# Output product with 4-column stationary loads, and heads 0 to 4 of wo loaded last, one transfer each

## The chip, the cores and the metric

One core of one Trainium2 chip. The metric is the device time of one execution in microseconds (us). A profiled or timed execution also has a *span*: from the first to the last of the program's own instructions, less than its time by 1.6 to 1.9 us in the kernel before.

## The reference

```python
# one decode step, batch 4, D = 448; 16 query heads on 8 KV heads, 8192 cached keys, head size 256
xn = layernorm(A_x)
q  = (xn @ wq)                                   # 448 x 4096
p  = softmax(q . k_cache / 16)                   # 32 pairs (batch, KV head): 4 MB of K and 4 MB of V each
o  = p . v_cache
s  = o.reshape(4, 1, 4096) @ wo                  # the "output product": 4096 x 448
g  = silu(B_ref(xn, w1, w2, w3, w4))             # a small MLP
out = A_x + s * g                                # 4 x 1 x 448, bf16
```

279 MB are read to compute 1792 numbers.

## The kernel before

One queue (SP, SyncE) issues all large loads in order: weights, K and V of 32 heads, and wo. Most of wo (`NLATE` and up) comes early; the heads in `LATE` come last, behind all of V. The last head's V comes in four pieces.

```python
LATE = ((0, 1), (2,), (3,))              # heads of wo at the end of the stream, by transfer
NLATE = sum(len(g) for g in LATE)
...
load_wo(NLATE, HQ, "dwo")                # early, between the first K loads
for h in range(2, NH):
    load_k(h); load_v(h - 2)
load_v(NH - 2)
load_v(NH - 1)                           # the last head's V, in pieces of 32, 16, 8, 8
for i, hs in enumerate(LATE):
    load_wo(hs[0], hs[-1] + 1, "dwl%d" % i)
```

At the end TensorE finishes attention and multiplies by wo. Heads `NLATE` to 13 are done while V still comes in (`f_ou`). The rest is this (`DQ` = 224, `NDG` = 2, `PQ` = 32, `Bn` = 4; OT holds the attention output with its 4 batch columns padded to 32):

```python
def f_o(hs, stop=False):
    for hq in hs:
        for dh in range(NHALF):
            for i in range(NDG):         # two groups of 224 columns: a "pair" of matmuls
                ins = pe.matmul(o_ps[i * PQ:(i + 1) * PQ, 0:DQ],
                                OT[:, hq // REP, hq % REP, dh, :],          # stationary, 32 columns
                                wo_sb[:, hq, dh, i * DQ:(i + 1) * DQ], ...) # moving, 224 columns
...
f_direct(NPIECE - 1).then_inc(S["p_pv"], 1)      # last piece of V; VectorE then writes the last OT
take(pe, "dwl0", 16)                             # wait for a landing
f_o(LATE[0])
take(pe, "v_ot")                                 # wait for the last OT (heads 14 and 15)
f_o(range(HQ - REP, HQ))
for i in range(1, len(LATE)):
    take(pe, "dwl%d" % i, 16)
    ins = f_o(LATE[i], i == len(LATE) - 1)
ins.then_inc(S["p_o"], 1)                        # VectorE: times silu, plus x; then the store
```

In each head's body TensorE transposes K, so it waits for K's landing at the top of the body. That is its one long idle stretch per head (28 such waits in the trace of before, 76.3 us together, the longest 4.6 us).

## Time and profile before

| | |
|---|---|
| time | 657.61 us median (657.61 to 658.3, 3 runs) |
| span of the profiled execution | 656.9 us |
| HBM | 278.99 MB, 425 GB/s over the span |

In the page's slices (the span in 40 equal parts, tenths of full) the DMA engines are busy at 90% or more from the second slice to the last but one.

```profile
PEclk9698999887899878889987888988878987887998
DMA  8999999999999999999999999999999999999996
```

So the load stream sets the pace, and only what comes after its end can be won or lost by an engine. The timeline of the last microseconds (start us, duration us, engine, line, operation; in brackets the idle time before it and what ended it):

```profile
649.21 0.55 PE L697 MATMUL pst<-pT,kn 128*128 128x32 bf16 x16 [0.19 <-PEq L245]
...
650.56 0.56 PE L697 MATMUL pst<-pT,kn 128*128 128x32 bf16 x16
651.27 0.18 DVE L520 TENSOR_TENSOR OT<-pst,rz 128x4 bf16<-128x4 f32 x1 [1.79 <-DVEq L245]
651.58 2.01 PEld L687 LDWEIGHTS pst<-wo_sb,OT 128*32 128x32 bf16 x24 [0.57 <-issue]
651.61 2.41 PE L687 MATMUL pst<-wo_sb,OT 128*32 128x224 bf16 x24 [0.50 <-PEq L245]
654.06 0.38 DVE L526 TENSOR_TENSOR res<-pst,sg 64x224 f32<-64x224 f32 x1 [2.61 <-PE pst L687]
654.47 0.38 DVE L528 TENSOR_TENSOR out_b<-res,x 64x224 bf16<-64x224 f32 x1
```

L697 is the direct product on the last two pieces of V, L520 writes the last OT, L687 is `f_o`. Its 24 matmuls end at 654.02. The chain that ended last consists of these and nothing earlier (start, duration, what):

```profile
651.61 2.42 PE pst L687 x24
...
654.06 0.39 DVE res L526
```

The DMA issues in the last 42 us: operation, KB, us from issue to landing; and the SP queue's timeline.

```profile
wo_sb<-in_A_wo_dram SPq DMA_DIRECT2D x1, 448.0 KB, 29.5
wo_sb<-in_A_wo_dram SPq DMA_DIRECT2D x2, 224.0 KB, 29.6
```

```profile
621.96 11.71 SPq L229 DMA_DIRECT2D wo_sb<-in_A_wo_dram  x3
```

The first of the three is issued at 621.96 and lands 29.5 us later, at 651.48; by the trace's landing records the others land at 652.03 and 652.59. Nearly all of the 11.71 us of issuing is the third issue (10.7 us). Seven earlier transfers had not landed even at its end, and no other issue on this queue took over 0.6 us. No record names the cause.

Last, busy times of the engines in two stretches. The third number from the end is TensorE's granted clock:

```profile
620.00:627.00 7.00, 5.88 (x92) 5.70 (x93) 2.59 (x5) 2.98 (x7) 0.00 (x0) 0.76 1.00 431
...
651.70:653.40 1.70, 1.70 (x20) 1.64 (x21) 0.00 (x0) 0.00 (x0) 0.00 (x0) 0.50 0.02 8
```

The output product ran at half clock.

### The profile page before, as it was taken

The page shows a single profiled execution, that of the slowest core. Times are in us where ns is not written, and L with a number is a line of the kernel's source. Part 1 is how long each engine was busy: PE and PEld are TensorE (multiplying, and loading weights), DVE is VectorE, ACT ScalarE, POOL GpSimd, SP SyncE. Part 2 cuts the span into 40 slices and gives each one's busy share as a digit, 9 for nine tenths or more (in the row PEclk, how much of TensorE's full clock was granted, in tenths as well). Part 3 has the DMA queues.
Part 4 walks back from the last instruction along what each step waited for, and adds up shares of the span by engine and source line. Part 5 has one row for each costly group of instructions (what it writes and reads, how often), then busy time and mean ns, then how long its engine had stood idle before and what let it go on. Part 6 is the DMA issues. An engine that isn't in the chain of part 4 may idle for free. (4 is left out here: it accounts for less than half of the span.)

```text
span 656.9 us, 22864 instructions
## 1 busy us (share of the span) xinstructions
PE 556.3 (85%) x9937; PEld 476.3 (73%) x9937; DVE 276.5 (42%) x589; ACT 256.0 (39%) x364; POOL 13.4 (2%) x77
## 2 busy tenths in 40 slices
PE   1899997988888988888897888898888889888897
PEld 0487886876766887667787766798767678766775
DVE  7353554443443444434443443444334443433442
ACT  4144544442433443323444333444333344433340
POOL 2000000000000000000000000000000000000000
PEclk9698999887899878889987888988878987887998
DMA  8999999999999999999999999999999999999996
GB/s 360 440 413 425 434 427 437 425 439 427 437 427 435 429 435 431 431 435 427 437 429 433 429 433 429 433 429 433 429 435 431 433 431 435 429 433 433 429 425 256
DMA packets 12353, 279.13 MB, mean 425 GB/s; under 512 B 1204, under 2 KB 3256, under 8 KB 3768
## 3 DMA queue, kind: packets, MB, share of 16 engines
q1 hardware_dynamic: 12328, 278.99, 99.2%
q8 instruction: 7, 0.11, 0.1%
q14 instruction: 2, 0.02, 0.0%
q10 hardware_dynamic: 16, 0.01, 0.0%
HBM read 278.99 MB, written 0.00 MB: 425 GB/s over the span
## 5 line engine op out<-in xcount | busy, mean ns | idle before, releaser
L588 PE MATMUL pst<-ident_b,kn 128*128 128x128 bf16 x4096 | 347.3, 239 | 78.6 <-PEq L245 76.3
L295 ACT ACTIVATE kT<-pst 128x1024 bf16<-128x1024 bf16 x224 | 229.3, 1024 | 360.6 <-ACTq L245 359.5
L588 PEld LDWEIGHTS pst<-ident_b,kn 128*128 128x128 bf16 x4096 | 275.4, 108 | 84.3 <-issue 83.8
L293 DVE COPY kT<-pst 128x1024 bf16<-128x1024 bf16 x288 | 197.5, 691 | 263.7 <-DVEq L245 263.7
L600 PE MATMUL psc<-qc,kT 128*128 128x2 bf16 x4096 | 178.7, 165 | 0.0
L600 PEld LDWEIGHTS psc<-qc,kT 128*128 128x128 bf16 x4096 | 157.7, 98 | 28.5 <-issue 28.3
L639 PE MATMUL psv<-vb,pT 128*4 128x512 bf16 x1056 | 86.4, 378 | 0.3 <-issue 0.3
L618 PE MATMUL psm<-sel,po 128*128 128x2 f32 x272 | 36.8, 257 | 0.5 <-PEq L245 0.5
L618 PEld LDWEIGHTS psm<-sel,po 128*128 128x128 f32 x272 | 34.8, 197 | 0.9 <-issue 0.9
L639 PEld LDWEIGHTS psv<-vb,pT 128*4 128x4 bf16 x1056 | 22.3, 82 | 15.3 <-issue 0.8
L452 DVE TENSOR_REDUCE rmax<-psc 128x2 f32<-128x128 f32 x32 | 9.3, 292 | 48.8 <-DVEq L245 48.8
L470 DVE COPY po<-psv 128x512 f32<-128x512 f32 x34 | 23.5, 692 | 3.0 <-DVEq L245 2.3
L457 DVE TENSOR_REDUCE gmax<-psm 2x1 f32<-2x128 f32 x32 | 8.9, 279 | 34.7 <-DVEq L245 34.7
L317 ACT ACTIVATE pT<-psc,negb 128x64 bf16<-128x64 f32 x66 | 20.6, 331 | 5.4 <-ACTq L245 5.4
L612 PEld LDWEIGHTS psm<-diag,ones_f 2*128 2x128 f32 x66 | 14.1, 263 | 6.4 <-issue 5.4
L280 POOL COPY qc<-qT 128x4 bf16<-128x4 bf16 x32 | 5.9, 186 | 585.8 <-DVEq L469 568.6
L612 PE MATMUL psm<-diag,ones_f 2*128 2x2 f32 x66 | 16.8, 321 | 1.1 <-PEq L245 0.9
L317 ACT ACTIVATION_READ_ACCUMULATOR pT<-psc,negb 128x1 f32 x66 | 13.6, 206 | 0.0
L608 PEld LDWEIGHTS psm<-ident_f,rmax 128*2 128x2 f32 x32 | 2.6, 80 | 14.0 <-issue 14.0
L536 PE MATMUL pst<-ident_b,xn_b 4*128 4x4 bf16 x14 | 0.6, 161 | 13.6 <-DVE xn_b L365 8.9
L630 PE MATMUL psm<-rowsum,ones_f 128*128 128x2 f32 x64 | 11.6, 251 | 0.0
L536 PEld LDWEIGHTS pst<-ident_b,xn_b 4*128 4x128 bf16 x14 | 0.5, 100 | 13.6 <-issue 8.9
(101 smaller groups left out, 122.4 us busy)
## 6 DMA issues: line engine op xcount, KB each, us to landing
kn<-in_A_k_cache_dram SPq DMA_DIRECT2D x32, 4096.0 KB, 25.7
vb<-in_A_v_cache_dram SPq DMA_DIRECT2D x31, 4096.0 KB, 31.3
vb<-in_A_wq_dram SPq DMA_DIRECT2D x1, 3584.0 KB, 11.7
vb<-in_B_w_dram SPq DMA_DIRECT2D x2, 1568.0 KB, 16.6
wo_sb<-in_A_wo_dram SPq DMA_DIRECT2D x1, 2688.0 KB, 44.3
kn<-in_A_v_cache_dram SPq DMA_DIRECT2D x1, 2048.0 KB, 25.2
kn<-in_A_v_cache_dram SPq DMA_DIRECT2D x1, 1024.0 KB, 27.3
kn<-in_A_v_cache_dram SPq DMA_DIRECT2D x2, 512.0 KB, 28.5
```

Source lines behind the costliest of these rows:

```text
L293: engine.tensor_copy(dst, src).then_inc(S["v_ev"], 1)
L295: engine.activation(dst, src, ACT.Copy).then_inc(S["a_ev"], 1)
L317: ins = act.activation(pv_p[:, :, hh], sc[:, :, hh], ACT.Exp, bias=negb[:, s, hh:hh + 1], scale=SCALE, accum_out=rowsum[:, s, hh:hh + 1])
L452: v.tensor_reduce(rmax[:, :], psc[h % 2][:, 0:NCH * REP].rearrange("p (k h) -> p h k", h=REP), AX.X, ALU.max).then_inc(S["v_rmax"], 1)
L457: v.tensor_reduce(gmax[:, :], psm[0:REP, 0:P], AX.X, ALU.max).then_inc(S["v_s"], 1)
L470: v.tensor_copy(po[:, slot], psv[:, 0:CP * DH]).then_inc(S["v_po"], 1)
L588: ins = pe.transpose(dst[:, t * P:(t + 1) * P], kn[:, h % 2, GC * j + kl, half * P:(half + 1) * P], ident_b[:, :])
L600: ins = pe.matmul(psc[h % 2][:, kk * REP:(kk + 1) * REP], kT[:, j % RING, t * P:(t + 1) * P], qc[:, h % 2, half, :], start=(half == 0), st ...
L612: pe.matmul(psm[:, P:P + REP], ones_f[0:REP, :], diag[:, :], start=True, stop=True).then_inc(S["p_m2"], 1)
L618: ins = pe.matmul(dst(dh)[:, 0:width], po[:, slot, i * DH + dh:(i + 1) * DH:NHALF], sel[:, i, 0:width], start=(i == 0), stop=(i == CP - 1))
L630: pe.matmul(psm[:, P + REP:P + 2 * REP], ones_f[:, :], rowsum[:, h % 2, :], start=True, stop=True)
L639: ins = pe.matmul(psv[o:o + CP * REP, 0:CP * DH], pT[:, h % 2, kk * REP:(kk + CP) * REP], src[:, kk:kk + CP, :].rearrange("p c d -> p (c d)"),
```

## The change

Two things. The output product loads 4 stationary columns in place of 32, the padding being zero. And head 4 of wo moves from the early load to the end, where five heads now come in a transfer each, so that the product can follow the landings head by head.

```diff
-    LATE = ((0, 1), (2,), (3,))
+    LATE = ((0,), (1,), (2,), (3,), (4,))
@@ f_o
-                            ins = pe.matmul(o_ps[i * PQ:(i + 1) * PQ, 0:DQ],
-                                            OT[:, hq // REP, hq % REP, dh, :],
+                            ins = pe.matmul(o_ps[i * PQ:i * PQ + Bn, 0:DQ],
+                                            OT[:, hq // REP, hq % REP, dh, 0:Bn],
```

`LATE[0]` runs ahead of the wait for the last OT, all else behind it. Before, `LATE[0]` was two heads, and 16 matmuls stood behind the wait (heads 14, 15, 2, 3). After, it is one head, and 24 stand behind it (14, 15, 1, 2, 3, 4).

## The prediction

> **What bounds the kernel now.** The load stream. The page's slices show the DMA engines at 90% or more from the second slice to the last but one, 425 GB/s over the span. So only the end counts; the chain of waits starts at 651.6 us of the 656.9 us span.
>
> The last transfers land (records of the trace) one behind the other: the last piece of V at 650.37 us, heads 0 and 1 of wo at 651.48, head 2 at 652.03, head 3 at 652.59. That is 1.11 us for two heads and 0.555 us for one: 224 KB at about 413 GB/s, with no visible fixed cost per transfer. The output product's 24 matmuls (the timeline's line L687) start at 651.61 and end at 654.02, so they outlast the last landing by 1.4 us. From 651.67 us the granted clock is 0.50, and a pair (two column groups of 224 columns, side by side) then starts every 187 ns.[...] The pair's pace is thus the moving operand's, not the weight load's.
>
> **Stationary loads of 4 columns.** [...]In the trace the loads (146 ns) are issued ahead and hidden; what shows is the stagger of 33 ns between the two matmuls of a pair; with 4 columns (attention's product has such loads) it is 3 to 4 ns. I expect the pace of 187 ns to stay and about 0.03 us to be saved, once, at the end.
>
> **Five transfers, one head each.** The bytes don't change; head 4 (224 KB) moves from the early bulk to the end. All K and V land about 0.54 us earlier (the last piece of V at 649.83). The steps between 640 and 651 us each start within some 0.1 us of a landing, so they move along, and the last OT (now 651.44) comes at about 650.9. The end of the stream stays at 652.6, or up to 0.1 us later for two more transfers. Head 0 is now done before OT is there; heads 14 and 15 run from 651.05 at the full clock (until it drops), heads 1, 2 and 3 soon after landing, and only head 4's two pairs remain after the last landing. After the last landing: 0.135 us to the first matmul (as before), 0.19 to the second pair, 0.39 for its latency: the product ends near 653.3, against 654.02. Were the clock at half from 651.05, twelve pairs would end at 653.55. Saved: 0.5 to 0.85 us, all on the critical path. The tail after it only moves.
>
> **Predicted time:** 656.9 us, range 656.0 to 658.0. Faster by over 2%: 0.01; within 2%: 0.98; slower: 0.01.
>
> **What would show it.** Last V piece 0.5 us earlier, last wo landing within 0.15 us of 652.6, landings of wo 0.55 us apart; 28 matmuls on the product's line, pace 187 ns at half clock with a stagger of a few ns; an idle gap on TensorE before the last heads, ended by a landing; end of the product near 653.3.
>
> **What would make it wrong.** The third wo transfer's issue already took 10.7 us[...]. Two more may stall longer; if the fifth is queued only after about 650 us the stream gets a hole and the end comes later. The clock may drop earlier. The runs before differ by 0.7 us, as much as the gain.

Three passages are cut from it, where marked: two rules that this case does not show, and a reading of the long issue. The forecast's sum came to 657.61 - 0.7 = 656.9 us. That the pace is the moving operand's, the traces show. At full clock, matmuls with 448 moving columns start 189 ns apart (L668 in before), groups of matmuls with 512 columns 216 ns (L639 in before) and pairs with 224 columns 95 to 96 ns (L687 in after), and below the pairs keep that pace with 32 stationary columns (e3) as with 4.

## The result

| | before | after |
|---|---|---|
| time, median (range), 4 runs each | 657.61 (657.41 to 658.3) | 658.03 (657.83 to 661.02) |
| span of the profiled execution | 656.9 | 656.1 |

The ratio of after to before is 1.0016, with a 95% interval of 0.9996 to 1.0035: the same. A ratio here is the mean time of one kernel's fast runs over that of the other's of the same rounds, so it is not quite the ratio of the medians. (One of after's four runs took 661.02; a later control has such a run of the kernel before too, 660.92.)

The time did not fall by 0.7 us, although the profiled execution's span is 0.72 us shorter. Of that, 0.51 us is the earlier end of the product (653.51 against 654.02). The other 0.21 us lies behind the product: from its end to the end of the span it is 2.83 us in the profiles with three transfers (before, e1, e4, e9 below) and 2.62 us in those with five (after, e2, e3, e10, e15). The times don't show this part, since time minus span is larger by about as much (on average 1.75 us in before, 2.06 in after, 1.99 in e3). e3, which keeps the 32 columns, shows that the five transfers bring it; why is not on record.

The page's slice line for DMA, and the timeline, of after:

```profile
DMA  8999999999999999999999999999999999999997
```

```profile
649.56 0.57 PE L697 MATMUL pst<-pT,kn 128*128 128x32 bf16 x16
...
651.17 0.56 PE L697 MATMUL pst<-pT,kn 128*128 128x32 bf16 x16
651.65 0.09 PEld L687 LDWEIGHTS pst<-wo_sb,OT 128*4 128x4 bf16 x4
651.66 0.36 PE L687 MATMUL pst<-wo_sb,OT 128*4 128x224 bf16 x4
651.88 0.18 DVE L520 TENSOR_TENSOR OT<-pst,rz 128x4 bf16<-128x4 f32 x1 [1.79 <-DVEq L245]
652.17 1.08 PEld L687 LDWEIGHTS pst<-wo_sb,OT 128*4 128x4 bf16 x24 [0.42 <-issue]
652.20 1.31 PE L687 MATMUL pst<-wo_sb,OT 128*4 128x224 bf16 x24 [0.19 <-PEq L245]
653.55 0.38 DVE L526 TENSOR_TENSOR res<-pst,sg 64x224 f32<-64x224 f32 x1 [1.50 <-PE pst L687]
```

The chain, the wo transfers, SP's timeline, and the same two stretches:

```profile
652.20 1.33 PE pst L687 x24
...
653.55 0.40 DVE res L526
```

```profile
wo_sb<-in_A_wo_dram SPq DMA_DIRECT2D x5, 224.0 KB, 29.1
```

```profile
621.22 17.97 SPq L229 DMA_DIRECT2D wo_sb<-in_A_wo_dram  x5
```

```profile
620.00:627.00 7.00, 6.50 (x77) 6.32 (x78) 2.14 (x4) 2.68 (x7) 0.00 (x0) 0.51 0.98 421
...
651.70:653.40 1.70, 1.51 (x30) 1.06 (x28) 0.18 (x1) 0.00 (x0) 0.00 (x0) 1.00 0.05 18
```

Compare step by step. The five wo transfers land 0.51 to 0.63 us apart and the last one at 652.62, against 652.59: as predicted. The last piece of V lands at 649.74, 0.63 us earlier than before: as predicted. The last OT, however, is written at 652.05, not at the predicted 650.9 but 0.6 us *later* than before. And the product's last 24 matmuls take 1.31 us where 24 took 2.41: the product's clock was 1.00 here and 0.50 before. The product ends 0.51 us earlier because it ran 1.10 us shorter at the full clock and started 0.59 us later, behind the late OT. The diff gives no reason why the clock should differ.

That led to three theories, which the expectations below call:

- **CLOCK.** The clock's half stretches fall at different places in each execution. With the clock at half in the product, the kernel before outlasts the last landing by 1.4 us; with the full clock it keeps up with the landings, and nothing is left to win. I predicted from an unlucky execution.
- **CHAIN.** The last OT comes late in some executions, and then the 24 matmuls behind it, against 16, cost time.
- **SPLIT.** Five transfers cost the stream time that I did not see.

### The profile page after: what moved, and what is told of

Same layout as the page of the kernel before. It is cut to its first block, busy times and chain, and to the rows that moved or that the text cites. A ratio compares the mean times of both kernels' runs of the same rounds, so it can differ in the third digit from the quotient of the medians.

```text
span 656.1 us, 22872 instructions
## 1 busy us (share of the span) xinstructions
PE 556.5 (85%) x9939; PEld 476.7 (73%) x9939; DVE 276.5 (42%) x589; ACT 256.1 (39%) x364; POOL 13.4 (2%) x77
## 5 line engine op out<-in xcount | busy, mean ns | idle before, releaser
L639 PE MATMUL psv<-vb,pT 128*4 128x512 bf16 x1056 | 86.3, 378 | 0.2 <-issue 0.2
L639 PEld LDWEIGHTS psv<-vb,pT 128*4 128x4 bf16 x1056 | 22.2, 82 | 15.2 <-issue 0.7
```

The costliest lines, as they stand in the source:

```text
L639: ins = pe.matmul(psv[o:o + CP * REP, 0:CP * DH], pT[:, h % 2, kk * REP:(kk + CP) * REP], src[:, kk:kk + CP, :].rearrange("p c d -> p (c d)"),
```

## The experiments

"Ratio" is to the kernel before, timed on the same chip in the same rounds. L is the landing of the last wo transfer.

### The two kernels again, and each half of the change alone

```diff
 e1_before_again: no edit          e2_after_again: the kernel after
 e3_late_only:  before, with
-    LATE = ((0, 1), (2,), (3,))
+    LATE = ((0,), (1,), (2,), (3,), (4,))
 e4_cols_only:  before, with
-    pe.matmul(o_ps[i * PQ:(i + 1) * PQ, 0:DQ], OT[..., dh, :], ...)
+    pe.matmul(o_ps[i * PQ:i * PQ + Bn, 0:DQ], OT[..., dh, 0:Bn], ...)
```

**e1_before_again.** 

> The kernel before, unchanged, as its own control. Three theories of why no gain was measured. CLOCK: the profile of before caught an execution whose product of 24 matmuls ran at half the TensorE clock (pairs 187 ns apart, end 1.4 us after the last landing); in executions where the clock is full there, the product keeps up with the landings and there is nothing to win. CHAIN: the work before the product (last head's scores, attention, direct product) ends later than the landings by an amount that differs by run, and the five heads after it pay for that. SPLIT: five transfers cost the stream time. Under CLOCK and CHAIN this profile differs from the one of before by up to 1 us in span, with another set of half-clock windows near the end; if the product runs at full clock it ends within 0.6 us of the last landing. Under SPLIT alone it repeats 656.9 us within 0.2. Timed: ratio 1.000 within 0.002.

**e2_after_again.** 

> The kernel after, unchanged, on the same chip. CLOCK: span and place of the half-clock windows differ from the first profile of after; the product's end follows the clock in it. CHAIN: the last piece of V lands near 649.7 us again, but the direct product on it starts 0.5 to 1 us after that landing. SPLIT: last wo landing later than in e1_before_again by more than 0.15 us. Timed: ratio to before 0.999 to 1.002; prediction's value would be 0.999.

**e3_late_only.** 

> Only the five transfers, stationary loads of 32 columns kept. All theories: within 0.002 of after, since the pace of a pair of matmuls is set by its 224 columns (187 ns at half clock, 93 at full). If the 4 columns are worth more than I think, this is slower than after by the difference. SPLIT: ratio to before above 1.000 by as much as after's.

**e4_cols_only.** 

> Only the stationary loads of 4 columns, three transfers as before. CLOCK and CHAIN: ratio to before 1.000 within 0.001; stagger in a pair falls from 33 to about 4 ns, pace of the pairs unchanged at the same clock. If the pace of pairs falls below 93 ns at full clock or 187 at half, my reading of the pace is wrong.

The 93 ns in the last two texts is an estimate of mine, half of the 187 ns that before's trace shows at half clock. For products issued twice, the later texts reckon with 187 ns at full clock and 373 at half in the same way.

| run | median us | ratio (95% interval) | profiled span |
|---|---|---|---|
| e1_before_again | 657.70 | 0.9998 (0.9985 to 1.0012) | 655.8 |
| e2_after_again | 657.85 | 1.0002 (0.9988 to 1.0015) | 655.6 |
| e3_late_only | 657.90 | 1.0000 (0.9987 to 1.0014) | 655.4 |
| e4_cols_only | 657.70 | 0.9998 (0.9985 to 1.0012) | 655.8 |

All four take the time of the kernel before, to within intervals of about 0.0014. The control e1, the *unchanged* kernel, has a span 1.0 us below the profile that I predicted from. Its product, in the timeline, and the two stretches:

```profile
651.52 1.48 PE L687 MATMUL pst<-wo_sb,OT 128*32 128x224 bf16 x24
651.74 0.17 DVE L520 TENSOR_TENSOR OT<-pst,rz 128x4 bf16<-128x4 f32 x1 [1.79 <-DVEq L245]
```

```profile
620.00:627.00 7.00, 6.22 (x79) 6.04 (x80) 2.14 (x4) 2.81 (x7) 0.00 (x0) 0.56 1.00 431
651.70:652.90 1.20, 1.20 (x24) 0.84 (x20) 0.17 (x1) 0.00 (x0) 0.00 (x0) 1.00 0.01 2
```

The same 24 matmuls with the same 32 columns took 1.48 us in place of 2.41, for the clock is 1.00. The product ends at L + 0.71, not within the 0.6 us expected, because the last OT came late (L - 0.38): CHAIN shows in the kernel before too. In e4, also three transfers, the product ends 0.49 us behind L:

```profile
651.51 1.47 PE L687 MATMUL pst<-wo_sb,OT 128*4 128x224 bf16 x24 [0.50 <-PEq L245]
```

And e2, the kernel after, does just what I had predicted of it: the last OT at 650.85, and a product that idles for the landings, with only head 4 behind the last.

```profile
650.45 0.36 PE L687 MATMUL pst<-wo_sb,OT 128*4 128x224 bf16 x4
...
650.67 0.17 DVE L520 TENSOR_TENSOR OT<-pst,rz 128x4 bf16<-128x4 f32 x1 [1.79 <-DVEq L245]
...
650.99 0.93 PE L687 MATMUL pst<-wo_sb,OT 128*4 128x224 bf16 x16 [0.18 <-PEq L245]
...
652.12 0.36 PE L687 MATMUL pst<-wo_sb,OT 128*4 128x224 bf16 x4 [0.20 <-PEq L245]
...
652.66 0.36 PE L687 MATMUL pst<-wo_sb,OT 128*4 128x224 bf16 x4 [0.18 <-PEq L245]
```

It ends at 653.01, L + 0.49: no closer to its landing than e4, which has none of the split. At full clock the work behind the last landing is the same in both (one head, two pairs), so both end at L + 0.49. SPLIT finds no support: L is 652.29 and 652.49 with three transfers (e1, e4), 652.52 and 652.25 with five (e2, e3). Taken alone, e2's landing is 0.23 us behind e1's, more than the 0.15 us that I had set as the sign of SPLIT; e3 and e4 differ by as much the other way, so it is scatter. The 4 columns change the stagger in a pair (at full clock mostly 14 to 17 ns in e3 and 3 to 5 ns in after, by the records of single matmuls; the 33 ns of before are at half clock) and not the pace: at full clock pairs start 95 ns apart in after (4 columns) and in e3 (32).

### Holding the clock

In the records of before and of after the clock changes only at points of a grid of 3.41 us. From 56 us on, the half stretches last 3.41 us (18 in before, 15 in after) or 6.83 us (10 and 12), but for the one in which each trace ends. The place differs by run: the last head's body meets a half stretch that starts at 620.95 in before and at 620.08, twice as long, in after. In the 3.41 us ahead of these stretches TensorE was busy for 0.04 to 0.61 of the time in before and for 0.00 to 0.54 in after; only the stretch in the product of before came behind a busier one (0.80). If idle waiting brings the half clock, which is my guess from this, filling the wait should remove it. So: small matmuls at the top of each body, into PSUM that is not in use there.

```diff
             def body(h):
+                for i in range(30):                                      # e5 to e8
+                    pe.matmul(psc[h % 2][0:PVW, 0:P], ident_b[:, 0:PVW], ident_b[:, :],
+                              start=True, stop=True)
                 for j in range(NGR):
 e7 and e8 also, in f_o ahead of each matmul: the same matmul into psc[h % 2][..., 256:480]
```

**e5_before_fill.** 

> The kernel before with 30 small matmuls put into TensorE's idle wait for K at the top of each head's body[...]. CLOCK: the half-clock stretches after the first heads vanish (last head's body and product at 1.00), the last OT is ready by about 650.9 us instead of 651.3 to 652.05, and the product ends 0.5 us behind the last landing; ratio to before 0.9990 to 1.0000, spread smaller than 0.9 us. If the fill does not hold the clock, or K waits for the fill, ratio 1.000 to 1.002.

**e6_after_fill.** 

> The kernel after with the same fill. CLOCK and CHAIN: with the clock full, both kernels end 0.5 us behind the same last landing, so e6 and e5 agree within 0.0005, in the timed ratio and in the time from last landing to the product's end within 0.1 us. My prediction's mechanism, if it held at full clock, would have e6 0.6 us (0.001) below e5.

**e7_before_fill_double.** 

> e5 with every matmul of the late output product issued twice, the copy into unused PSUM: pairs 187 ns apart at full clock, as the profile of before had them at half clock. CLOCK: the product now ends about 1.3 to 1.5 us behind the last landing, as in that profile: 0.8 to 1.0 us later than in e5.

**e8_after_fill_double.** 

> e6 with the same doubling. CLOCK: the gain I predicted shows here: the product ends 0.5 to 0.8 us behind the last landing, 0.5 to 0.9 us (0.0008 to 0.0014) before e7. If the last OT is late (after 651.6), the 24 matmuls behind it cost more than the 16 of before and e8 is no faster than e7: that would be CHAIN.

Measured: 662.15, 662.01, 662.93 and 663.46 us; ratios 1.0066, 1.0062, 1.0077 and 1.0100. All are slower by more than the noise (no interval reaches 1), though by 1% at most: a miss, and of the experiment's own making. In e5 the page's DMA queue of kind instruction (packets, MB, share) and TensorE's timeline show it:

```profile
q8 instruction: 16, 0.26, 0.2%
```

```profile
324.97 0.27 PE L608 MATMUL psm<-ident_f,rmax 128*2 128x128 f32 x1
339.25 3.20 PE L648 MATMUL psc<-ident_b 128*32 128x128 bf16 x30 [14.01 <-issue]
```

Before has 7 such packets, of 16 KB each; e5 to e8 have 16. TensorE stood still for 14.01 us in mid-run in e5, and in the 22nd of the page's 40 slices the stream moved 413 GB/s (363 in e6), against 433 in before. The stall's cause is not named by any record; that it belongs to the added packets is my estimate from their coming together. 16 packets in place of 7 are what the texts below call a second fetch (of the loop). The times of e5 to e8, so disturbed, say nothing about the change. What stands within each profile: at full clock and with an early OT, e5 ended at L + 0.51 and e6 at L + 0.49; the doubled pair e7 and e8, whose last OT was late (0.2 and 0.5 us ahead of L), ended at L + 1.86 and L + 2.10, so after was no better there.

The mended fill is seven long matmuls per body, 28 instructions in the loop:

```diff
             def body(h):
+                for i in range(7):
+                    pe.matmul(psc[h % 2][0:PVW, 0:4 * P], ident_b[:, 0:PVW], kT[:, 0, 0:4 * P],
+                              start=True, stop=True)
                 for j in range(NGR):
 (and a memset of that part of kT at the start)
```

**e9_before_fill7.** 

> e5's idea mended.[...] Here seven matmuls of 512 columns per head fill the wait, 28 instructions in the loop. No second fetch and no 14 us stall expected; K and V landings 9.71 us apart throughout. CLOCK and CHAIN: clock 1.00 from 615 to 653 us, last OT 1.1 us or more ahead of the last landing, product ended 0.5 us behind it. Ratio to before 0.9988 to 1.000.

**e10_after_fill7.** 

> After with the same fill. CLOCK and CHAIN: last OT 1.6 us or more ahead of the last landing (0.5 us more than e9, as predicted for the earlier V), and still the product ends 0.5 us behind the last landing as in e9: the earlier OT buys nothing, e10 and e9 agree within 0.0005. The prediction at face value: e10 0.0008 to 0.0013 below e9.

Measured: 657.97 us, ratio 0.9999 (0.9981 to 1.0016), and 657.95 us, ratio 1.0000 (0.9984 to 1.0017). No second fetch (7 packets each). In these two profiles the fill held the clock of the last body (it did not always: e12 and e13 below each have a half stretch of 3.41 us between 622 and 628). e9, two stretches and its product:

```profile
620.00:627.00 7.00, 6.57 (x129) 6.10 (x128) 3.56 (x7) 4.58 (x8) 0.00 (x0) 1.00 0.96 412
651.70:652.90 1.20, 1.20 (x18) 1.19 (x15) 0.00 (x0) 0.00 (x0) 0.00 (x0) 0.50 0.00 1
```

```profile
651.34 2.16 PE L691 MATMUL pst<-wo_sb,OT 128*32 128x224 bf16 x24 [0.53 <-PEq L245]
```

e10, the same:

```profile
620.00:627.00 7.00, 6.13 (x127) 6.04 (x127) 3.22 (x6) 4.57 (x8) 0.00 (x0) 1.00 0.99 426
651.70:652.90 1.20, 0.99 (x16) 0.35 (x12) 0.00 (x0) 0.00 (x0) 0.00 (x0) 1.00 0.16 60
```

```profile
650.85 1.50 PE L691 MATMUL pst<-wo_sb,OT 128*4 128x224 bf16 x20
...
652.56 0.36 PE L691 MATMUL pst<-wo_sb,OT 128*4 128x224 bf16 x4 [0.21 <-PEq L245]
...
653.12 0.36 PE L691 MATMUL pst<-wo_sb,OT 128*4 128x224 bf16 x4 [0.20 <-PEq L245]
```

Both last OTs are now as early as predicted (L - 1.18 and L - 1.78, so 0.6 us apart). In e9 the clock dropped in the product nevertheless, and it ended at L + 1.19, as the first profile of before had shown; my expectation of L + 0.5 assumed the full clock there. e10 ended at L + 0.50. Here are the two cases of the theory side by side in one pair, but the times are equal, and in the two profiles e10's stream happened to end at 652.98 and e9's at 652.31. That scatter of the stream from run to run is as large as the gain.

### A slow product at a known clock

To see the predicted gain without depending on where the clock drops, I made the product slow on purpose: every matmul of `f_o` twice, so that a pair takes an estimated 187 ns at full clock (measured in e11: 191).

```diff
 in f_o, ahead of each matmul, on top of the fill of seven (after has 0:Bn and its rows accordingly):
+                            pe.matmul(psc[h % 2][i * PQ:(i + 1) * PQ, 2 * P:2 * P + DQ],
+                                      OT[:, hq // REP, hq % REP, dh, :],
+                                      wo_sb[:, hq, dh, i * DQ:(i + 1) * DQ], start=True, stop=True)
 e13, e14: five matmuls of fill; e16, e17: seven, f_warm(4) dropped, and in e17 head 0 not doubled
```

**e11_before_fill7_double.** 

> e9 with every matmul of the late product issued twice (the copy into unused PSUM): at full clock a pair then takes 187 ns, what it takes at half clock without the copy. With L for the last landing: the product starts 0.98 us before L (heads 0 and 1 land together), twelve pairs follow at 187 ns, so it ends at L + 1.4 us, within 0.15. If the clock drops to half in the product, the pair takes 373 ns and the end is later; the pace says so.

**e12_after_fill7_double.** 

> e10 with the same doubling. CLOCK: this is the case that I predicted for. Last OT at L - 1.7, head 0 before it, twelve pairs after it: the product ends at L + 0.8 us, within 0.15, so 0.6 us less behind the landing than e11. If e12 is no closer to its last landing than e11, the mechanism of the prediction is wrong even at this pace, not only its assumed clock. The timed ratio can hardly resolve 0.001.

e11: 658.64 us, ratio 1.0017 (1.0001 to 1.0034). L = 652.36 (TensorE stood still for 6.57 us near 326 us, but the landings kept their pace), last OT at L - 1.18, clock 1.00, pairs 191 ns apart, product ended at 653.89: L + 1.53. A product at this pace does cost the kernel before about 1 us of time (median 658.64 against 657.64). e12: L = 655.95, last OT at L - 1.69, clock 1.00, product ended at 656.88: L + 0.93, 0.60 us less behind its landing than e11, the amount expected for this pair and within the 0.5 to 0.85 us of the prediction. The starts of VectorE's first step behind the product, e11 and then e12:

```profile
653.92 0.38 DVE L527 TENSOR_TENSOR res<-pst,sg 64x224 f32<-64x224 f32 x1 [2.74 <-PE pst L695]
```

```profile
656.92 0.38 DVE L527 TENSOR_TENSOR res<-pst,sg 64x224 f32<-64x224 f32 x1 [2.66 <-PE pst L695]
```

Its time is spoilt again, though: 661.62 us, ratio 1.0054 (1.0038 to 1.0070), with 16 instruction packets. Two attempts to get a clean time followed.

**e13_before_fill5_double.** 

> e11 with five matmuls of fill in place of seven. No second fetch of the loop. Product's end at L + 1.5 us (L: last landing), timed ratio to before 1.0012 to 1.002, as e11.

**e14_after_fill5_double.** 

> e12 with five matmuls of fill. If no second fetch: product's end at L + 0.9 us, and the median 0.4 to 0.8 us below e13's; its ratio to before 1.000 to 1.001. If it isn't below e13's although its profile ends closer to L, something else in after costs what the product saves.

e13: 659.59 us, ratio 1.0030 (1.0016 to 1.0045), L + 1.51 as expected, the ratio above the 1.0012 to 1.002 expected. e14: 663.74 us, ratio 1.0084 (1.0064 to 1.0103), 16 instruction packets, and the product ended at L + 2.51. Failed.

**e16_before_double_short.** 

> e11 without the four fill matmuls that follow the last head's body. No second fetch. Product's end at L + 1.5 us, median as e11's, 0.7 to 1.1 us above the kernel before.

**e17_after_double_short.** 

> The same for after, head 0 not doubled. If it fetches its loop once only: product's end at L + 0.9 us, median 0.3 to 0.9 us below e16's. If it fetches again, its time says nothing and only the distance to its own last landing stands.

e16: 658.80 us, ratio 1.0012 (0.9999 to 1.0025). e17: 660.47 us, ratio 1.0037 (1.0016 to 1.0057), without a second fetch. But here the clock dropped within the last 40 us in both (to half for 6.83 us from 639.4 in e16, from 621.6 and again from 642.1 in e17, where the long fill then runs at half clock as well). The last OT came at L - 0.03 in e16 and L + 2.42 in e17, and the products ended at L + 2.05 and L + 5.03, not at the L + 1.5 and L + 0.9 expected; so both profiles are cases of CHAIN, and the times compare late OTs, not the split. I have no clean time of a slow product in after. What is shown of the mechanism is shown within traces: before and e9 (L + 1.43, L + 1.19), e11 and e13 (L + 1.53, L + 1.51), against e12 (L + 0.93), the one profile of five transfers with a slow product and an early OT.

### The matmuls behind the last OT

```diff
 after, with
-                take(pe, "dwl0", 16)
-                f_o(LATE[0])
+                for i in range(3):
+                    take(pe, "dwl%d" % i, 16)
+                    f_o(LATE[i])
                 take(pe, "v_ot")
                 f_o(range(HQ - REP, HQ))
-                for i in range(1, len(LATE)):
+                for i in range(3, len(LATE)):
```

**e15_after_order.** 

> After, with heads 1 and 2 of wo ahead of the wait for the last OT: 16 matmuls behind it, as before the change. CHAIN: when the last OT is late (within 0.7 us of L) the product ends by L + 0.6 us in place of L + 0.9 us; when it is early, at L + 0.5 as ever. Timed: 0.9992 to 1.0003 of before, not to be told from after.

658.05 us, ratio 1.0001 (0.9988 to 1.0014). The last OT was at L - 0.84 and the product ended at L + 0.49:

```profile
651.40 1.73 PE L687 MATMUL pst<-wo_sb,OT 128*4 128x224 bf16 x28
```

As expected, but a weak test. The rule of the next section gives L + 0.62 for after's own order at this OT, so the reorder saved an estimated 0.13 us in this execution, and the timing can't show that. No experiment points to a version that would beat both kernels by more than the scatter of the runs.

## Why the prediction was wrong

All profiles of plain or filled kernels with the product issued once and the stream intact. The clocks are those of the stretches shown above (620 to 627 us, and the product); the landings, the OT and the product's end are from the trace's records. Distances are differences of rounded times and can be off by 0.01.

| run | LATE | clock, last body | last V lands | last OT | OT behind V | L | clock, product | product's end |
|---|---|---|---|---|---|---|---|---|
| before | 3 | 0.76 | 650.37 | 651.44 | 1.07 | 652.59 | 0.50 | L + 1.43 |
| e1 | 3 | 0.56 | 650.04 | 651.91 | 1.87 | 652.29 | 1.00 | L + 0.71 |
| e4 | 3 | 0.76 | 650.27 | 651.34 | 1.07 | 652.49 | 1.00 | L + 0.49 |
| e9 | 3 | 1.00 | 650.06 | 651.13 | 1.07 | 652.31 | 0.50 | L + 1.19 |
| after | 5 | 0.51 | 649.74 | 652.05 | 2.31 | 652.62 | 1.00 | L + 0.89 |
| e2 | 5 | 0.76 | 649.69 | 650.85 | 1.16 | 652.52 | 1.00 | L + 0.49 |
| e3 | 5 | 0.60 | 649.44 | 651.35 | 1.91 | 652.25 | 1.00 | L + 0.58 |
| e10 | 5 | 1.00 | 650.12 | 651.20 | 1.08 | 652.98 | 1.00 | L + 0.50 |
| e15 | 5 | 0.56 | 649.79 | 651.79 | 2.00 | 652.63 | 1.00 | L + 0.49 |

At full clock one rule, made from these same profiles, gives all of the last column to within 0.03 us: the product ends at L + 0.49 (0.135 from landing to first matmul, 0.095 to the second pair, 0.26 for its latency), or at the last OT + 0.15 + 0.095 for each pair behind it after the first + 0.26, whichever is later. For e1, with 8 pairs, that is L - 0.38 + 1.08 = L + 0.70; for after, with 12, L - 0.57 + 1.46 = L + 0.89.

Point by point:

1. **The stream binds, and its end does not move: right.** L is 652.3 to 652.6 with three transfers and 652.3 to 653.0 with five. The longer issuing (17.97 us in place of 11.71) cost nothing: the last issue was through at 639.2, 13 us before that transfer landed.
2. **V lands 0.54 us earlier: right.** The last piece lands 2.22 to 2.25 us ahead of L with three transfers, 2.81 to 2.88 with five.
3. **4 columns are worth 0.03 us at most: right in the traces.** The pace of the pairs is 95 to 96 ns with 4 columns and with 32; the timings (e3, e4: some 0.9 us either way) can't resolve 0.03 us. In the records a load takes at full clock about 97 ns for 32 columns (e1), 80 to 85 ns for 4 (e4).
4. **"The steps between 640 and 651 us each start within some 0.1 us of a landing, so they move along": wrong as a rule.** Even in the trace that I had, the attention product of the head before last started at 641.33, 0.9 us behind its landing at 640.41. The table shows what this rests on: with the last body's clock at 0.76 or more the OT is done 1.07 to 1.16 us behind V, with 0.51 to 0.60 it takes 1.87 to 2.31 us, because TensorE is then late itself (after starts the direct product at 649.56 on a piece that landed at 648.46; before at 649.21 on one of 649.07). The fill supports the clock as the cause: in both filled kernels the body's clock is 1.00 and the figure is 1.07 and 1.08. The spoiled profiles agree: 1.07 to 1.15 in e5, e6 and e11 to e14, which meet at most one half stretch of 3.41 us there, and 2.30 in e8, which meets one of 6.83 us. In the two profiles of after the OT came 1.15 us too late once, and on time once (652.05 and 650.85, predicted 650.9).
5. **"Saved: 0.5 to 0.85 us, all on the critical path": the step that failed.** Its largest term was the 1.4 us by which the product outlasts the last landing. I read it from one trace and took it for the kernel. It belongs to executions whose product runs at half clock: L + 1.43 and L + 1.19 there. At full clock the three transfers of before are already at L + 0.71 (e1) or L + 0.49 (e4), and after is at L + 0.49 to L + 0.89, so there is nothing to win, and with a late OT four more pairs to pay for, an estimated 4 x 0.095 = 0.38 us.
6. **The sum mixed two executions.** I took 0.7 us, a difference measured in a span of 656.85, from 657.61, the median of other runs. Of the 64 timed runs of the kernel before that were made beside the experiments, the median span is 656.15 us and only 5 have 656.9 (as the list rounds) or more. The profile was of an execution among the slowest tenth. Counted from its own span the forecast would have been 656.85 - 0.7 = 656.15; the profile of after has 656.13. That agreement is luck: 0.21 us of it is the shorter end of the span, which the time does not show, and the rest is the clock, not the split; the median run of the unchanged kernel has 656.15 as well.

CLOCK is thus what the runs support for most of the missing gain: the control e1 and e4 show that the overhang is absent at full clock, e2 and e10 that the earlier OT then buys nothing, and e11 and e12 that at half the pace some 0.6 us are there, in one pair of traces. That the timed runs were mostly at full clock in the product is inferred: they record only the mean clock of the whole execution. CHAIN is real but smaller (e1, after's first profile, e3). SPLIT has no support: L differs by no more between the two kinds than within each.

What stays open: the clock was at half in the product in 2 of the 5 profiles with three transfers and once-issued matmuls (before, e9; not e1, e4, e5), and in none of 6 with five (after, e2, e3, e6, e10, e15). Both of the two had an early OT; the four plain profiles with a late OT (e1, after, e3, e15) all had the full clock in the product, so the two losses were not seen together. Whether five transfers keep the clock up or this is chance, I can't say; the drop came in both cases at 651.65 to 651.67 us, where after's clock grid has no point (650.80 and 654.22 are the nearest). Nor does a single timing exclude an average gain or loss of 0.5 us: e2's interval is 0.9988 to 1.0015. But none of the five kernels with five transfers and an unspoiled stream leans towards the predicted 0.9989: after, e2, e3, e10 and e15 have ratios of 1.0016, 1.0002, 1.0000, 1.0000 and 1.0001.

## What to carry to other kernels

Before you cost a saving from a trace, ask whether that execution is typical: compare its span with the spans of other runs, and look at the granted clock in the very stretch that you want to shorten. If the work at a stream's end outlasts the last landing only at half clock, as here (L + 1.43 against L + 0.49), a split that lets it follow the landings earns nothing when the clock is full; what counts then is the work behind the *last* landing, and here that was one head of wo before and after. Compare times with times: a span can shrink (here by 0.21 us) without the time. And when you take work out of the group ahead of a wait, count what now stands behind that wait.

## What else these runs measured

- The granted clock drops for 3.41 or 6.83 us again and again in a kernel that is bound by loads (mean granted clock 0.89 to 0.90), at another place in each execution. The same 24 matmuls took 2.41 us in one execution (before) and 1.48 us in another (e1). The clock of one stretch late in a kernel, read from one profile, need not be typical.
- Filling TensorE's waits raised the mean clock from about 0.90 to 0.96 and did not change the time (e9: ratio 0.9999), since the load stream binds; a fill of more instructions, with 16 instruction packets, made the kernel slower (e5: 1.0066).
- By an estimate from the edits, at two instructions a matmul, programs of up to 76 instructions more than before had 7 instruction packets (e11), those of 80 and more 16 (e14). With 16 came a stall of 14.01 us on TensorE in e5, and e5 to e8, e12 and e14, which all have 16, are 4 to 6 us slower than the kernel before.
- Transfers of 224 KB, queued one behind the other, landed 0.555 us apart, which is 413 GB/s, against 432 GB/s for 4 MB (9.71 us); five in place of three moved the end of the stream by nothing that shows.
